# H3 convolution plus gated MLP, forward and gradients: the recorded order of all instructions and their PSUM banks replaced

## The chip, the cores and the metric

The kernel runs on one core of one Trainium2 chip. The metric is the time of one execution in device microseconds (us), given as the median over runs. One more execution is recorded by the hardware profiler, and views of its trace are quoted in what follows. A core has the engines PE (TensorE, matrix multiplies and transposes), DVE (VectorE), ACT (ScalarE), POOL (GpSimd) and SP (SyncE), which here issues all the DMAs; 16 DMA engines carry them.

## The reference

A token sequence x of length S = 2048 and width D = 512 (bf16) goes through a layer norm, and two blocks are added to it. Wanted are the result and its gradients for nine inputs. Shortened:

```
def _A_ref(q, k, v, shift_k, ssm_k, ssm_D):
    # k_shift: sum over t = 0..3 of k_pad[:, t:t+S] * shift_k[:, 3-t]
    kv = k_shift * v
    # FFTs of length 2S in float32 over the sequence
    y = irfft(rfft(kv_pad) * rfft(ssm_k_pad))[:, :S]
    return q * (y + kv * ssm_D)
def _B_ref(x, w_gate, w_up, w_down):
    return ((x @ w_gate) * (x @ w_up)) @ w_down

x = A_q
xn = _layernorm(x)
out = x + _A_ref(xn, A_k, A_v, A_shift_k, A_ssm_k, A_ssm_D) + _B_ref(xn, B_w_gate, B_w_up, B_w_down)
# returned: out, and the gradients of sum(out * grad_out) for A_q, A_k, A_v,
# shift_k, ssm_k, ssm_D, w_gate, w_up, w_down
```

The hidden width is F = 1376.

## The kernel before, in words

**Layout.** The sequence is held as 16 rows r of 128 tokens, one token on each partition. Nearly all of SBUF is one tile, `big`, in which every array has a fixed address; all of PSUM is one tile, `PP`, cut into eight banks. Therefore the profile calls nearly everything `big` or `PP`. Four arrays in DRAM carry results between stages: HD (products of the MLP), AX (first step of the transform), CX (spectral product) and KS (shifted k).

**How the order is made.** The kernel's text does not issue instructions itself. The engines are replaced by the wrapper `Eng` (lines 143 to 179), and each call is appended to a list `ops` of 2,285 recorded operations: 1,009 for PE (several matmuls can be one operation; 3,190 in all), 654 for DVE, 361 for ACT, 3 for POOL and 258 for SP. PSUM is asked for in 398 slots (`rF` for two banks, `rN` for one) without a place. At the end `emit(PLAN)` (lines 181 to 189, called on line 976) decodes the string PLAN of line 34: 2,285 numbers, the order in which the operations are really issued, and 398 numbers, the bank of each slot. Line 173 is the wrapper's inner line, so nearly every instruction of the profile carries L173. Each engine runs its own instructions strictly in the issued order; semaphores between engines follow from the data. The calls `at(t)` note a due time beside each operation; with a given PLAN they decide nothing. All DMAs are on SP's queue, so an SP instruction that waits holds up all later loads and stores.

**Stages, in the order of time.**

- Start (0 to 34 us): dummy matmuls (324 to 334), then loads, from 362 on: rows of x (`xload`), the transposed gradient goT (`gtload`), the first weights (lines 363 and 367; the other groups by `w_load`, 321), and the gradient `go` in four pieces of four rows (`gload`). `ln` (392) normalizes, `tr_rows` (406) transposes.
- `mlp_rows(j, r)` (416): for six column groups j of F and pairs of rows r, the product pd of go and W_down, the products with W_gate and W_up, and their pointwise products. These stay in a ring in SBUF and mostly go to HD (`hd_store`, 443). `dw_gen(j)` (582) makes the weight gradients of group j from them.
- `a_gen` (453): the shift convolution on DVE and the first step of the transform on PE, stored to AX. `s_gen` (`s_B` 514, `s_pw` 529, `s_Bi` 546): over the frequency blocks, loads of AX and of tables E into SBUF, the spectral products on DVE, the way back, stores to CX. Both are interleaved with the MLP, up to about 240 us.
- `turn_gen` (615): the last two column groups don't go through HD. They are transposed in SBUF, partly by eight DMAs (`ldT`, here called turn(r) by its row), partly by PE in groups numbered k = 0, 8, ... 88.
- `hd_load(n)` (642): a DMA transpose from HD, once for each n = 0 to 7.
- The late loop, n = 0 to 7, two rows each (from 240 us to the end; lines 935 to 975). For each n, `c_load(n)` (676) loads the block C from CX (1.5 MB), and `last_dft(n)` (719) is the last step of the transform on PE; `c_y` (729), `c_dkv` (737) and `c_o5` (755) work on its three results. `c_dsk` (764) forms products on DVE and adds them up on PE; `dk_pair` (710) is the transposed shift convolution, seven DVE operations and a store. `y_o(n, rr)` (784) is the MLP's last product for row 2n + rr, 11 matmuls with what `hd_load(n)` brought, added to the rows of x (`y_load`, 688), then a store of out. `y_x(n, rr)` (801) is 22 matmuls, the layer norm's gradient on DVE and ACT, and a store of the gradient of x. `k_load` (691) and `dkv_load` (682) bring rows of k, v and KS. `psd_end` (824) copies and stores the sums of `c_dsk`.

So there are three kinds of chains in the late loop: CX by DMA to `last_dft` and on to ACT and DVE; HD by DMA to `y_o` and `y_x` and on to DVE; and buffers of one or two turns, which a store must have left before DVE writes them again, and which a load must not overwrite before PE and DVE have read them.

The line that plays the recorded operations is this:

```
            for i in order:
                for fn in ops[i].fns:
                    fn()
```

Of the kernel before, what the change touches and what calls it, by code (L numbers as in the profile page):

```python
# [17 lines left out]
S = 2048  # L18
D = 512
F = 1376  # L20
R = 16
# [4 lines left out]
SB = [0, None, 1, 2, 3, 4]  # L26
# [4 lines left out]
RING = 28  # L31
RO = [0, 16, 24, 40, 56, 72]
EPS = 1e-5
PLAN = "c-l=@V-TK6vu*dpcCx|7wr$(C?G1Kgd$Swcwr$(Cv$pS>e1C2|T~jkXjdS{`nw|m307-zM7^Hwtpa>)YflN>w;zMFc2nflcC@2^>1c(ArAsUo`=nw-+LNbU6r6Cq1f>O{H+Cv$L4RIg`#D%g@4pPEOhzB`gCgg%u&<;94M@R*EAs;k@7Vs4$h1`%D@<S(R37Me)6ofo50=hs~C<Ha3Gc<w1&>WgVZRiHIpgYuoDliBpLtUr@RiPeKhEJgZ42CJt5Gp_`7z3lAA`FE3@EKHtk<bWwKzW!5LtrRWhuts<j=&<=1dZVf*aDx!XjlwmVHj+N*3bviz*gu93m`iThpCVWGvhYc4%1*E?15{L7<<7{NP;_|DkjBhI0L4`myis1z%Iyw)o}^*g{9CNYG79U4#vSUSPrwHAN(cX!W`%iE8uIG1#4k7T!M9w7LLL9Fc*G+bg%}}!wL8mqT@VR4?n_j7!N051MG(^Z~(5uDaeL<;U_o;w_qRKhU9n<Qs5!@1b>F?cp6gTWk`j;z<Ch-1|CCdOoJET23&+s@hYUn9GDK%<4wqbSKvNmgpBwQa^e$s1T`@iD&|JR2apy11xLVuwXilK=D{{l2kYYRkQbw1KFp8x@HeQB|3Lvf3s0dSM#To$5dVO?PzW30GHi^?aRsi#KcN|}!oQ(8w!oIy3ZFw0{0my+Mp%b2a2O89JMaS9U^HBfZLu9T#b?kSW8xazjeBqu#=;KR5j$aL9F1Kt4(>(98t@uk!an?4-auCzfv;d3#>Q+g690kq*d4p!J9rBda3YSu{Wu+a;3VvcYq1y3z}`3>Cu1KRi(lae{2Hg=0o;fOu`f==e%K#3;{d!%pV2^EfSd3$jEi65JRF1zaSjf~AvhNY(EvDtg>fbh#d|Ox2h)6LL7!thT!gc6F}9>xco^$bLM(y}s3<n11Q;J%QC%8BOR*8Pre@THwqQLvgdM3dHK(K4iHhMAI*!Hh1eU;(*q%z^G3-D?sSTCJQ<w<L;2AuRgctB4mc`R}7R%u!yo}{>8eYNA=?l7w74U1Sh}W<ZR>qUql&)hHyn#1yE5@W9cnfdi9lVRNs4abg_i!r3rZ^Or?&CCifDiE$#iK{~7^l-N+>TH1DL%valz^UNLP|t4=mmaBeJCa6q+B$RwqYttO)oJqy~0w|m(tKVEKM`%HNL?zl$-vPb~Kz$QywZyd8r)rpnUWe-{E^a14-ypN=xM_9aW&D^bLNCBPcy(pfmIx=BMv5BPF8(l!-D^Mfw4M#Gfz={fxihub7nzQa1VxlT#t8M8D%%`U4A7cKQ>0(l9zlJMl048~?!+^e_I0MW`rMreXwyM8s5ugeJfeR5Eg^N}o`mYV;LVrzljMa!^z%LD8r))u5VGlA==`I#08y3tgaE)Qx)49GXijX&&{at~8QX(J0zL>!=@%rh7Do)>D64N@M9hZKUP&fR@oXdPpm16Rn}~G?6CLCE87^X#(w}!?1_8(<7Qhn`sw)OIv6M?WG0u9qps7^dnuQh4d4hq{Xy|=F|7|10ACGaD*PyVR}k8=w~`gOXvXIrduTZ3q7Hmbdc^uNGgBIX_@&MrQ`Jck}_~cenHPE6ThO&{2Q&M%XE#7(eIRnv+{AeLfQB#W#_*r2mehu+4(iSrCdCS-_Uh>N4XjJJ;i0@cpQWCu<;)>nE#|9JdOXQp*)47@xSs9ea`<#dH#Z9a(o`f(K!ka=X^Yg$8rLW%9D9C$Ku#rfh+P<p3Y;q5+`KS{9J&?@kp-BLAQ}B=qOIai8=C%bUY{Ff?S2aq5q^17iQK8Jcq0DEGoiDxi-ZhQPo)-MU(MdPR`La1xM4bcs~{8VqBb~YE1o_XLAgVqn~g!j;9?tu9o1Gnvzp-Nsh0nwK~_}QXETTYbs66rMV0bpfsF76KYvbqcyo4C)Q6jktWr=T#Gw#60Oa3IISkvx|~kaYdub;ow*Bl<rLbD>vMO`rWv#WH{|TvgFn$YoL?JpPj1XjxGCpQf)SikoADyft@C*;H|LBxk8^2d{gT&l6>Y%<bOyKNUfhaX^J4DJRW-9_)jnKU7jhO|#+h^p=hfxBl>2f)t*Lpm9~aVE`jTI9F>S*ov@I9WqFP+nb8UUi8@QBK(;C{Hs%uFtqh+-}x8v)4gUe}Yy~($D0O!-&TwdGr9j>4abs*Q#N_v+&aAUp4_xS<8;YRw9D{3pPr*C-$KjH@Zm|N=;uCGt|8Mo0U`i`G-Gi|FK^gVyWb@f~Rj@xMxNh%Y$pElL@noK(B_uN90OA6_t1N0N=s4F?8^w-YXLkDYD9il^Z6Q`2YvW<Ic8ri|y`7{1hy6X=-P=Dl|oK|}4XWCr1@K2mh2I*G*TvzjM?xt(FmyXoYnnQMRHtD13rLT_CNt#_UNJ|}~Ipt^0DC2apZsaVIRWeB~`Gt$fuRK<#X;E3M$9SpcmJ@WGPw+`T#Y^-w57RSTLeBDV4KiJ)>aX;ruHq>=LTBiH4qQ^c(kL=ZqslTpzz2DzF4r$~g+`M(T1?LI0$r)&b%I8hLtI?u>3P1uG30Aqq-%7x9^sg>N-uJ0i6!%OweHqSyiot6b$Xc>@Lb)izwut)pjUVwU*+}sJ5SWuvPDbDF1^NE^$$MG+cb{kk!rF>YselxsClKj9M+n$QRB){-lPR&zi!ri5>F23K0TyYw6+}8{1RXO<bskwu4zIkEQw?@&*Z<jiX@h+dPFa3RoSk8^Cdm5JM|ylp=IQ<p3{H%g5J>cx>gIxX+5T8<*fe4C$xf`(sEK!&ge}ADK9PLme!J!`c!Xg6G3Sycl4Rw)$7_+?rCLtq0OY8G>}TtT<+@|eWI<TzBH7F`dDA-EqS1=<&nPA=Xy=P(Z~@ezv^xIUF*n8eZfD;Z+cyB$ZHk(PH)OvRry1ImcO*FbdkpLr@mK{HsaDw?#j2?NdDHJ^hdoT?IpAPqyOs9`ipjz|FoNQkQeg3{vtnUM*({&ZH276Jd@~#)<evmOEl{#Zk?o;^p==*PlB;M61Dph*E&ld=_@fz?199$I2P3&OB73E52c^PvtQ+vd}?X!H|Z|}WT3p3&m@)&l9V=BVp{@BXh$TqCABGXRE|j^J1(g#oh7#9c0x`{5=(DW<&-3|X);|h*eCWxGTLc5Be!jaq_DH{rR23tmf5mcew!&-?JGGaU(0!!CE0DZJhD7i(6U($`%W&%Qz>jYEuZDG&63;Z$U7M#cdV!tw{K*q+_H;uNebELGFRrw_i|Z&mn~A-idX@gFAJokeJjOmkzA2dcF(?$5?02_+Avux3+263w&Ai>s#tk@Y};hJRJ9SZM3zc9+aWt;nJkxTwnA1)4I3$=<c;i->bBoT%PMJOZ)J?EmI_wU#>zNpYvZMowX+E_QPxO%t8KewkL;D2*1<a3B&lVcY_j|)ovn_|ve|au*2+3rFZ<+y{bOBhzig1M_Jee@x^~yPTRl4<2c?J2vHG@A=2`>$LpI4FX=sgXj2)K7*3)`f6KiU{t(i5q7S_jF+B}<Yt!%8dwgtA(#@Q1aZ%^&2Ot3{Z(car6n{3bQds}TUtgrR6pKOh-wQsDyEw&}L&VIB3Hqe&Z6#L8$*&thQ%WSYMx2ZPGHrNoGZpUnfeP<7Cg$=ch_N8sI&GxN5x0klXKDU{+(vI6#w$<L+HrsAL+ZVROhS}Hl&W77z`@u%oP8(^z*(w`luWgr&w%={Hy|O))+SB+S_O~T<_fNf;UoiGREx33zkK)lCojko4cl8)v!ee@3KV?z<FFRtfJcD1f*#3)|pSGix*7JKD&*+)FfbX@;9@oJOdlJv$l{~(mv6B9)U9+s7!?XDbYwc&PnwRo;UfpYW3jf4QdjhZNZ!Ej#^Xt~eJ9tj-=mkBQ|7+<ymlyI{-pR{&XK(9`y|$mUgkIKjds9#3dAyG2^}1fv%XxWk;uXBI*Yi}K+>3Y@@9I;$qPO#@-p!|ZPw(#2y}eiU{@%a`_~)L|2l@=3;5V#__wX-#nEz+<yqOR7rM}8P^D#c$>w81*<-L8GkMITF&l~v=@8hd|tS|Sz-rR56IlE*deU!KI%l4(O@tHo(XL$?%%2)VWAMN9Pov-)jzQKq3L~rRE{k(nclYEyS@)y3_H~UN9<nw*9zw&*4(BJq<f9tdTtZ(tHe$Nm4LVxEceU88PZ~US!@<D#YkNPD)<vV?!&GiR<%uo9gU+mxdHs9gLeY-#O{l3R9`w9Qf&-elV-mmy$zv|aKR!AFu@aulVfAVww%wM~QTmHM>^e3J!gb+L2_Bi3Z#|;-eeR$+iLcH)_<Pje~{OA}mg**PUKlKbDYDf_N@VlNc{NkBIqVT6v$Qbr|lE5KLxbM-zKb|!t4!?S~AmKMp6+Q`Vf`*i#Mko+0{N>R@(vUr*4sFAy;a~sTlZ6<eU`QTnhFT$J$Pr40+M!*@8R~@Gp>C)Ua)tJxV#pKfg%Y7s$Q$a1j-hgB5K4tYAzvsR3Wr9aOz0G<gkqs{IAC2u*^nl54GlwzaK)}#xzHjM3Hd|S&@FTi<-_FAAxsI4!{|^gG!Ml?|1dR-3DZK4Fd%#$dWDvuXQ&>UgrQ-2=pDWYGs4)=DtsB5hCX3)7#9YHnPFJi5<UxGg{@&-=o_|$;bDB36^4WnVSX4Hz7Ffd>@X@!2;0MsaL}5Cg<)dY8J30(VM%Bm_JrGESLhcGhGk)QI2MkF<za7F5sHR8VP!ZGPKE_xRk$1Wg;QZtSRGD>x#3FK8198L;eJ>Y28FX>UKku6gv()nxEdaYIbm@)6b^*L;Zb-Ku7$_pe7GLoh9}`^I1<i<O<_%V8J>lA;YN5BE`-<NXt){HhKu2Scph$rOW{R8Gt|gU9yoGwW^oh{^GG`rj!cZzoy~>aNIr-O2@s(}#1nu$a({J>EI;Za5*f@R@z9vuBGEr;h~R@eL>^g&2u>VvMx%%#(p)26CXt)FC@Y%6hvptxMzVuK<ak1jq|=BQlVL=KE)cP{NJmGAKr&E^I7cQCEf|VNoIi-0VkG?kzKGDrj2}Q6eI)dO&PP%fffzCRIDRxBh){z6|9#N?Z#RPZBVYR%#v}Cu`j8ngQpO1K50oO%B3mD7<q-_>0W*K7P=rckC6UT~2okALBvQoLKU7rz4<RIx`T"
KB = 1024


# [1 line left out]
def kernel(  # L39
# [141 lines left out]
    def emit(plan):  # L181
        raw = zlib.decompress(base64.b85decode(plan))
        order = struct.unpack(f"<{len(ops)}H", raw[:2 * len(ops)])
        for s, b in zip(slots, raw[2 * len(ops):], strict=True):
            s.base = Q[b // 2] if s.n == 2 else halves[b]
        with tc.manual_schedule(engines={mybir.EngineType.PE, mybir.EngineType.DVE, mybir.EngineType.Activation, mybir.EngineType.Pool, mybir.EngineType.SP}):
# [3 lines that stand above are left out]
# [452 lines left out]
    def hd_load(n):  # L642
        a, b = hd_span(n)
        ldT(out=hdP[n % 2][:, :, 0:b - a], in_=HP[n, a:b])
# [290 lines left out]
    for n in range(NCH):  # L935
# [32 lines left out]
        else:  # L968
# [4 lines left out]
            if n + 2 < NCH:  # L973
                y_load(n + 2)
                hd_load(n + 2)
    emit(PLAN)

# [106 lines left out]
```

## Time and profile before

| what | value |
|---|---|
| median of 3 runs | 427.12 us (426.57 to 427.43) |
| the profiled execution | 426.92 us, its span 425.1 us |
| PE busy | 414.8 us, 98% of the span |
| DVE busy | 350.7 us, 82% |
| ACT busy | 257.8 us, 61% |
| DMA moved | 127.27 MB, mean 299 GB/s |
| granted PE clock | 1.00 of full speed |
| last matmul ends | 420.1 us |

The span is the time from the first to the last recorded event; the 1.8 us between it and the profiled execution's time lie outside the trace. "Busy" counts the time in which an engine executes something, without its waits for semaphores; SP has no busy time, since issuing a DMA isn't counted. A wait is put down to what released it: "PE PP L173 <- DMA big<-CX" is a wait of PE, writing to PP, for a load from CX into `big`. The chain is the list of work that ended last, followed backward from the last instruction, each piece with what released it.

### The profile page before, as it was taken

What the parts mean: (1) busy time and instruction counts of PE and PEld (TensorE: products, weight loads), DVE (VectorE), ACT (ScalarE), POOL (GpSimd) and SP (SyncE); (2) the same over time, 40 slices, a digit from 0 to 9 for tenths busy, and PEclk for the clock granted to TensorE, in tenths of its full rate; (3) what the DMA queues carried; (4) which work ended last, traced back from release to release, by engine and by line L of the source; (5) the groups of instructions that cost most, each with busy time, mean ns of one, the idle gap of its engine ahead of it and who ended that gap; (6) DMA issues with size and microseconds to landing.
All of it is one profiled execution on the core that took longest, in us unless ns stands there. A gap on an engine that the chain in (4) does not pass through costs nothing.

```text
span 425.1 us, 8146 instructions
## 1 busy us (share of the span) xinstructions
PE 414.8 (98%) x3190; PEld 198.9 (47%) x3190; DVE 350.7 (82%) x684; ACT 257.8 (61%) x364; POOL 3.5 (1%) x9
## 2 busy tenths in 40 slices
PE   7999999999999999999999999999999999999995
PEld 4745555854554333544444334444444444444343
DVE  5999977998649989899999980325858898999996
ACT  4855988598644999888999953363414230422323
POOL 1000000000000000000000000000000000000000
PEclk9999999999999999999999999999999999999999
DMA  8999899999788879969889899999999999999953
GB/s 277 399 180 395 295 305 395 344 363 360 298 297 304 320 250 338 310 202 341 305 286 349 291 313 314 250 392 309 188 296 305 308 258 333 309 303 290 278 174 147
DMA packets 104222, 127.27 MB, mean 299 GB/s; under 512 B 63860, under 2 KB 73977, under 8 KB 103160
## 3 DMA queue, kind: packets, MB, share of 16 engines
q1 hardware_dynamic: 104184, 126.75, 94.4%
q8 instruction: 25, 0.41, 0.4%
q14 instruction: 13, 0.11, 0.1%
HBM read 57.10 MB, written 54.04 MB: 261 GB/s over the span
## 4 chain that ended last, share of the span: by engine, by line
PE 70%; DVE 14%; DMA 11%; issue 2%; ACT 2%; SPq 1%; ACTq 0%
PE PP L173 70%; DVE big L173 14%; DMA out_dram<-big 4%; DMA big<-CX 2%; DMA big<-in_k_dram 2%; ACT big L173 2%; SPq L173 1%; DMA big<-in_w_dram 1%; DMA big<-in_go_dram 1%; DMA big<-in_x_dram 1%; ACTq L1080 0%
## 5 line engine op out<-in xcount | busy, mean ns | idle before, releaser
L173 PE MATMUL PP<-big 128*128 128x512 bf16 (+7 forms) x3190 | 414.8, 351 | 5.3 <-DVE big L173 1.8
L173 DVE TENSOR_TENSOR big<-big 128x1024 bf16<-128x1024 bf16 (+2 forms) x465 | 268.1, 630 | 45.8 <-ACT big L173 36.7
L173 PEld LDWEIGHTS <-big 128*128 128x128 bf16 (+3 forms) x3190 | 198.9, 97 | 221.0 <-issue 64.4
L173 ACT CAST big<-PP 128x512 bf16<-128x512 f32 (+2 forms) x314 | 224.3, 781 | 87.1 <-PE PP L173 75.5
L173 ACT ACTIVATE big<-big 128x512 bf16<-128x512 f32 (+3 forms) x30 | 19.1, 642 | 50.1 <-DVE big L173 50.0
L173 DVE CAST big<-PP 128x512 bf16<-128x512 f32 (+1 forms) x37 | 32.4, 875 | 9.7 <-PE PP L173 5.1
L173 ACT COPY big<-PP 128x1024 bf16<-128x1024 bf16 x15 | 15.0, 1012 | 20.9 <-PE PP L173 20.8
L173 DVE SCALAR_TENSOR_TENSOR big<-big 128x1 f32<-128x1 f32 (+2 forms) x52 | 25.3, 499 | 0.3
L173 DVE SCALAR_TENSOR_TENSOR big<-big,PP 128x512 f32<-128x512 bf16 x14 | 9.6, 682 | 8.6 <-PE PP L173 8.6
L173 DVE BATCH_NORM_STATS2 big<-big 128x6 f32<-128x512 bf16 x16 | 10.5, 683 | 3.7 <-DMA big<-in_x_dram 3.7
L173 DVE TENSOR_TENSOR big<-big,PP 128x512 bf16<-128x512 bf16 x14 | 9.2, 681 | 1.1 <-PE PP L173 1.1
L173 DVE TENSOR_SCALAR big<-big 128x1 f32<-128x1 f32 (+1 forms) x28 | 6.8, 256 | 0.0
L173 POOL MEMSET big<- 128x1536 bf16 (+2 forms) x3 | 2.9, 950 | 252.3 <-PE PP L173 252.3
L173 ACT ACTIVATE big<-PP 128x512 f32<-128x512 f32 x2 | 1.2, 597 | 4.5 <-PE PP L173 4.5
L173 DVE BATCH_NORM_AGGREGATE big<-big 128x2 f32<-128x6 f32 x16 | 2.3, 169 | 0.1
L173 ACT ACT_TABLE_LOAD x1 | 1.3, 1283 | 0.7 <-PEq L1072 0.7
L173 DVE RECIPROCAL big<-big 128x2 f32<-128x2 f32 (+1 forms) x9 | 1.2, 151 | 0.6 <-ACT big L173 0.6
L173 DVE DVE_READ_ACCUMULATOR big<-big 128x1 f32 x16 | 1.3, 82 | 0.0
L173 DVE DVE_READ_ACCUMULATOR big<-big,PP 128x1 f32 x14 | 1.1, 81 | 0.0
L173 DVE MEMSET big<- 128x128 bf16 (+1 forms) x2 | 0.2, 112 | 0.8 <-PEq L1072 0.8
L173 DVE COPY big<-PP 128x1024 bf16<-128x1024 bf16 x1 | 0.7, 692 | 0.2 <-PE PP L173 0.2
L173 ACT ACTIVATION_READ_ACCUMULATOR big<-PP 128x1 f32 x2 | 0.4, 194 | 0.0
(6 smaller groups left out, 0.9 us busy)
## 6 DMA issues: line engine op xcount, KB each, us to landing
HD<-big SPq DMA_DIRECT2D x32, 384.0 KB, 5.8
AX<-big SPq DMA_DIRECT2D x16, 768.0 KB, 5.6
big<-AX SPq DMA_DIRECT2D x16, 768.0 KB, 5.5
CX<-big SPq DMA_DIRECT2D x16, 768.0 KB, 5.1
out_dram<-big SPq DMA_DIRECT2D x44, 256.0 KB, 3.5
big<-CX SPq DMA_DIRECT2D x7, 1536.0 KB, 8.3
big<-in_vK_dram SPq DMA_DIRECT2D x8, 512.0 KB, 5.3
big<-in_w_dram SPq DMA_DIRECT2D x4, 768.0 KB, 7.4
```

Of the source, the lines that this page charges most:

```text
L173: o.fns.append(lambda: f(*[fix(x) for x in a], **{kk: fix(x) for kk, x in k.items()}))
```

## The change

One line differs, the string PLAN (here cut after 60 characters of some 5,000):

```
-PLAN = "c-l=@V-TK6vu*dpcCx|7wr$(C?G1Kgd$Swcwr$(Cv$pS>e1C2|T~jkXjdS{`...
+PLAN = "c-lQ!W7wWYupZCGPGehbY&EuxHnyF#aT?pUZ6}Rw+fHqt_scog`LX-VHG9v@...
```

Decoded, the two strings hold the same 2,285 operations in two orders. The orders on PE, ACT, DVE and SP differ; that of POOL's three operations doesn't. 299 of the 398 PSUM slots have another bank. Operations, operands, SBUF addresses, tile shapes and the queue of each DMA are the same, and the large stages follow each other as before; what differs is the place of single operations within some microseconds on each engine. On average an operation stands 2.7 us of work from its old place on PE, 1.9 us on DVE and 1.6 us on ACT. The largest shifts:

- At the start SP issues x(2), goT(3), x(1), the first part of the weights, goT(1), x(0), goT(4, 5) and so on (numbers are rows, or pairs of rows for goT); before, x(2), x(6), goT(4, 5), x(0), D, the weights. One of the four pieces of `go` comes 17th instead of 27th. The first products on PE are pd of `mlp_rows` for r = 6 and r = 2; before, the transposes of row 2.
- PE's transposes of `turn_gen` come later: groups k = 32 to 64 by 16 to 35 us, 80 by 64.5, 88 by 78 us.
- `y_o(5, 0)` and `y_o(6, 1)` come later on PE (by 7 and 12 us of work). The last piece of PE's work is `c_dsk(7)`. The sums of `y_o(3, 0)` and `y_o(5, 0)` on DVE come later by 6.9 and 10.6 us.
- On SP, `hd_load(2)` stands four places earlier and `c_load(3)` seventh behind it instead of fifth; the store of `y_x(1)` and the DMA transpose turn(8) stand just ahead of `hd_load(4)`, the latter instead of just behind it; turn(14) goes from the 244th place to the 224th.

2 lines of the change are left out of this document (1 added, 1 removed).

## The prediction

> **What bounds the kernel now.** I read, in this order, the totals, the waits of each engine, the table by stage, the chain, and SP's instructions in order of time. The first two say that TensorE is nearly full and that its visible waits are short (after the name: us in total, times, longest):
>
> ```profile
> span 425.1 us, 8146 instructions
> PE 414.8 (98%) x3190; PEld 198.9 (47%) x3190; DVE 350.7 (82%) x684; ACT 257.8 (61%) x364; POOL 3.5 (1%) x9
> ```
> ```profile
> PE PP L173 <- DVE big L173: 1.8, 2, 1.1
> PE PP L173 <- DMA big<-CX: 1.7, 2, 0.9
> PE PP L173 <- DMA big<-in_w_dram: 0.9, 1, 0.9
> PE PP L173 <- DMA big<-in_go_dram: 0.6, 1, 0.6
> ```
>
> In the trace PE stands still for about 1 us at 6.8 (w), 32.2 (go), 335.8 (C), 363.1 (DVE), 380.2 and 395.2 (C); its matmuls without those and smaller gaps take 413.4 us. I count PE by this nominal time, and by its lag, the real time less the nominal one: 3.8 us from 34 to 300, then 4.6, 5.2, and 6.6 at the end. A new order can win nearly only from this lag, and can lose anything.
>
> ```profile
> 180.00:240.00 60.00, 60.00 (x615) 25.62 (x614) 59.42 (x111) 55.98 (x72) 0.00 (x0) 1.00 0.85 302
> 270.00:285.00 15.00, 15.00 (x99) 7.05 (x99) 4.98 (x8) 7.77 (x11) 0.00 (x0) 1.00 1.09 338
> 360.00:380.00 20.00, 19.27 (x112) 8.37 (x110) 20.00 (x44) 5.76 (x7) 0.00 (x0) 1.00 1.10 328
> 380.00:400.00 20.00, 18.93 (x138) 8.09 (x138) 19.93 (x43) 7.29 (x8) 0.00 (x0) 1.00 1.13 279
> ```
>
> In this table by stage (window; us, then busy of PE, weight load, DVE, ACT, POOL; clock, DMA share, GB/s) DVE has two thirds of a stage free at 270–285 and nothing from 360 on, and the DMA engines are full throughout the late loop. Per pass of that loop PE needs some 16 us, DVE 17.9, and SP's queue this:
>
> ```profile
> 372.84 10.67 SPq L173 DMA_TRANSPOSE big<-HD  x1
> 383.56 1.48 SPq L173 DMA_TRANSPOSE big<-big  x1
> 385.13 2.37 SPq L173 DMA_DIRECT2D out_dram<-big  x4
> 387.60 0.72 SPq L173 DMA_DIRECT2D big<-CX  x1
> 388.37 0.64 SPq L173 DMA_DIRECT2D big<-in_vK_dram  x1
> 390.65 0.33 SPq L173 DMA_DIRECT2D big<-in_x_dram  x1
> 391.08 9.50 SPq L173 DMA_TRANSPOSE big<-HD  x1
> ```
>
> The eight hd_loads (transposes from HD) hold SP for 7.3 to 10.8 us each, a plain issue for about 0.45. The trace also shows eight DMAs in flight at most: the issue at 336.8 comes with the landing, at 336.7, of the one eight before it. So three engines are within 2 us of each other, and the late end is set by SP's order: the chain ends with c_load(7), 387.60 to 396.42, then 23.7 us of PE without a gap, and 5.0 us of tail.
>
> **The change, part by part.** It is a permutation: no instruction is added or removed, all durations stay, so every term is a wait. The sum is against the profiled execution (426.92 us; span 425.1, 1.8 outside it), which is 0.20 below the median. I decoded both orders and laid the durations of before on the new one.
>
> *Start (0–34).* the first part of w_load(0) goes to SP's fourth place instead of its sixth, 896 KB of loads up to and with it instead of 1,409; the rows of go that stalled PE at 32.2 go 17th instead of 27th; the first real matmuls are pd of mlp_rows for r = 6 and 2. This takes the two stalls of 1.08 and 0.96 away; the later x(6) and x(8) give some 0.7 of new waits by the loads' landing rows. So PE is −1.3 at 34 us (bounds −2.0 and 0). What is late next is C in the late loop, which hangs only partly on PE, so I let −0.5 of it reach the end.
>
> *Middle (34–270), with the banks.* PE is busy 66.00 of 66, 80.00 of 80 and 60.00 of 60. Placed in the new order with the old times, s_B(0) comes 1.0 to 1.6 us before its E and X are ready near 126, and a bank that has changed asks in some ten places for an ACT copy 0.1 to 0.6 us too early. Most is made good by ACT's own shift. Nothing here could be gained, as there are no stalls left. I take +0.5 (0 to +2). On banks the Trainium skill ("Perfetto Trace Analysis", Matmuls) has independent groups rotate through different banks so that evacuation overlaps. Of the 398 slots 299 change bank and both orders rotate over all eight; by the rule this term would be 0, and the sum 0.5 lower.
>
> *Turn transposes, later.* The PE transposes of turn_gen that are in groups k = 32 to 64 go 16 to 35 us back, k = 80 and 88 64 and 78 us, each 0.45 us. PE then reaches the late items 2 to 4 us of work sooner: last_dft(3) at a nominal 314.3 instead of 316.6, (5) 356.7 for 358.8, (6) 370.8 for 374.5, (7) 388.5 for 389.9, y_x(7,0) 395.2 for 399.3. That would be a gain if PE could start them. But before, last_dft(3) started 0.29 us behind the landing of its C, and last_dft(4) 0.04 behind. So the gain turns into waits for C and HD.
>
> *SP, late.* I walked SP's new order with 0.45 per issue, the old holds, and landings by nearest rows (2.3 to 2.8 us behind an hd_load, 8.3 for a C load, 11.6 for hd_load). hd_load(2) stands four places earlier and goes at 298.9 instead of 300.8, c_load(3) comes seventh behind it instead of fifth. Issue times: c_load(3) 310.2 (before 311.7), hd_load(4) 341.4 (338.8, since a store that waits for DVE and the DMA transpose turn(8) now stand ahead of it), hd_load(5) 358.6 (358.0), c_load(6) 369.6 (368.2), hd_load(6) 373.4 (372.6), c_load(7) 387.0 (387.4), hd_load(7) 391.1 (390.8). The lag that each landing asks of PE: hd_load(4) 6.4, hd_load(5) 6.6, c_load(6) 7.2, hd_load(6) 6.9, c_load(7) 396.0 − 388.5 = 7.5, hd_load(7) 7.5. The end lag is then 7.5 instead of 6.7: +0.8, PE's end at 420.9 instead of 420.1. In other words, c_load(7) lands 0.4 sooner, but 24.9 us of PE work follow it instead of 23.5.
>
> *Heads of the queue.* Each hold could slip: the y_o(3) store (its DVE work goes back 6.9 us) stands ahead of hd_load(5), the y_o(5) store (back 10.6) ahead of hd_load(7). At 360–400 DVE has nothing free to catch up with. Behind those hd_loads on SP wait C and k for the next pass. My walk has 5 us of room for the second and about none for the first. Bounds 0 and +5; I take +0.9, a quarter of the 3.5 us by which the holds themselves differ, as the rows are nearest to no slip. On these holds a rule speaks against counting them: the Trainium skill ("DMA: Bandwidth & Descriptors", Issuing engines are not separate DMA queues) says the sequencer's time to initiate a DMA "is usually small relative to the DMA itself". The rows disagree (9.50 of some 11.6 us). By the rule this term would be 0, and the sum 0.9 lower.
>
> *DVE and tail.* One product of c_dsk(0) (1.28 us) goes into the hole at 270–285, and c_y's last product waits less for the y_x store (2.0 us at 320.6), so DVE is 1.5 to 2 us ahead at 322 and 0.9 when the x rows of y_load(3) gate it. PE's last item is c_dsk(7), behind it an ACT copy of the sums and a small store; DVE's chain for the last y_x ends about 0.6 sooner. Tail 4.6 instead of 5.0: −0.4 (−1.0 to +0.5).
>
> Sum: −0.5 + 0.5 + 0.8 + 0.9 − 0.4 = +1.3, so 428.2 against the profiled run and 428.4 against the median.
>
> **The rivals.** *Faster:* DVE, not SP, sets the late end. DVE is 90 to 100% busy there, and its lead of 1.5 to 2 us at 322 would then pass to the end, with the stores and hd_loads that wait for it. It decides at whether y_load(3) lands before 335 (my walk: 336.9). Against it stands the chain, which ends over C. −2 us: 425.1; chance 0.30. *No change (within 0.2%):* the C loads hold both orders to the same end; +0, 427.1; 0.18. *Much slower:* the store ahead of hd_load(4) or (5) waits for DVE, the hd_load slips by 2 to 3 us twice, and as SP has 8.3 + 7.2 + waits of each 17.9 us, it doesn't come back: +4 to +6, 432; it decides from a slip of 2 us, the room that DVE's lead gives; 0.20. *That the change does nothing:* all four working queues differ and 299 banks; only POOL's three operations keep their order. Left out.
>
> **How the numbers follow.** The forecast, 428.4, has 0.32; its own range is 427.9 to 429.5. A measurement can tell about 0.2% (0.85 us) from no change: faster 0.30, same 0.18, slower 0.52. The range takes in most of the faster case, down to 424.9, and of the much slower one up to 432.5; about a fifth is left outside.
>
> **What would show it.** Start: PE's waits for w and go gone from its list, PE ahead by about 1 us at 34. Middle: PE busy under 80.00 of 80. Late: PE's waits for C and HD longer (4 us or more instead of 1.7), hd_load(4) issued at 341 or later, the chain ending over C or HD. Tail: 4.6 us. I am wrong if DVE's waits shrink and PE's lag at last_dft(7) is under 6.6 (the faster case), or if SP's wait for DVE just ahead of an hd_load is over 2 us (the much slower one).

## The result, and the profile after

| what | before | after |
|---|---|---|
| median | 426.85 us (4 runs beside it) | 440.27 us (4 runs) |
| ratio | | 1.0307, interval 1.0273 to 1.034 |
| the profiled execution | 426.92 us, span 425.1 | 439.03 us, span 437.2 |
| last matmul ends | 420.1 us | 433.4 us |
| from there to the end | 5.0 us | 3.8 us |

The kernel became 13 us slower, outside the range of the prediction, and the profiled executions differ by 12.1 us. PE ends 13.3 us later; the tail gave 1.2 back. Executions that were disturbed (one of after's four) are left out of the ratios, and changes in microseconds are worked out from the ratios, though the medians hold them.

The page's totals of after:

```profile
span 437.2 us, 8074 instructions
PE 414.5 (95%) x3132; PEld 200.7 (46%) x3190; DVE 359.1 (82%) x684; ACT 257.4 (59%) x364; POOL 3.5 (1%) x9
```

The instructions are the same (58 matmul records are missing from this trace, hence x3132). ACT's busy time is as it was, but DVE's is 359.1 instead of 350.7 us with the same 684 instructions. That line turned out to be the key to a part of the loss. PE's waits over the whole span (us in total, times, longest):

```profile
PE PP L173 <- ACT big L173: 6.4, 7, 1.9
PE PP L173 <- DMA big<-CX: 4.1, 3, 2.7
PE PP L173 <- issue: 2.1, 12, 0.3
PE PP L173 <- DVE big L173: 1.7, 3, 1.1
PE PP L173 <- DMA big<-in_go_dram: 1.3, 1, 1.3
```

The first line is new: before, the list has no wait for ACT. The stage from 180 to 240 us, whose row of before the prediction shows, is now this (window; us, then busy of PE, weight load, DVE, ACT, POOL; clock, DMA share, GB/s):

```profile
180.00:240.00 60.00, 59.01 (x596) 26.85 (x607) 57.78 (x102) 53.40 (x70) 0.00 (x0) 1.00 0.79 277
```

In 180–240 PE, DVE and ACT all do less than before in the same time, so none of them is simply fuller: they hold each other up. The same table has the stage that lost most ahead of 240, first before, then after:

```profile
100.00:180.00 80.00, 80.00 (x703) 35.32 (x701) 65.95 (x109) 61.34 (x81) 0.00 (x0) 1.00 0.87 311
```
```profile
100.00:180.00 80.00, 76.84 (x642) 33.67 (x652) 65.67 (x106) 58.20 (x78) 0.00 (x0) 1.00 0.84 299
```

By PE's lag (the prediction's measure: real time less nominal time of the matmuls issued so far) the loss is spread. After less before is +0.5 us at a nominal 30 us, +2.2 at 100, +4.5 at 220, +8.2 at 250, +8.1 at 270, +10.4 at 320, +14.1 at 330 and +13.3 at the end. So about a third arises up to 220, more than a quarter in one short stretch (a nominal 220 to 250; in real time 244 to 261 us), and the rest between a nominal 285 and 330, which is about 298 to 349 us in real time. From SP's queue around its last two hd_loads, answering the list shown of before (start, us, what):

```profile
387.68 8.59 SPq L173 DMA_TRANSPOSE big<-HD  x1
400.44 0.41 SPq L173 DMA_DIRECT2D big<-CX  x1
404.02 9.04 SPq L173 DMA_TRANSPOSE big<-HD  x1
```

hd_load(7) goes 13 us later than before, and c_load(7) 12.8: the late loop as a whole is shifted. The chain no longer ends with 23.7 us of PE behind c_load(7). Behind a last piece of PE it ends with 26 us of DVE alone (408 to 434 us), of which the first piece stands here, so DVE, not a load, closes the kernel:

```profile
403.10 4.92 PE PP L173 x22
408.05 2.40 DVE big L173 x6
```

### The profile page after: what moved, and what is told of

It reads as the page before. It is cut to its first block, busy times and chain, and to the rows that moved or that the text cites. A ratio compares the mean times of both kernels' runs of the same rounds, so it can differ in the third digit from the quotient of the medians.

```text
span 437.2 us, 8074 instructions
## 1 busy us (share of the span) xinstructions
PE 414.5 (95%) x3132; PEld 200.7 (46%) x3190; DVE 359.1 (82%) x684; ACT 257.4 (59%) x364; POOL 3.5 (1%) x9
## 5 line engine op out<-in xcount | busy, mean ns | idle before, releaser
L173 PE MATMUL PP<-big 128*128 128x512 bf16 (+8 forms) x3132 | 414.5, 352 | 18.9 <-ACT big L173 6.4
L173 DVE TENSOR_TENSOR big<-big 128x1024 bf16<-128x1024 bf16 (+3 forms) x465 | 275.0, 632 | 48.6 <-ACT big L173 35.9
L173 PEld LDWEIGHTS <-big 128*128 128x128 bf16 (+4 forms) x3190 | 200.7, 98 | 232.2 <-issue 70.1
```

Of the source, the lines that this page charges most:

```text
L173: o.fns.append(lambda: f(*[fix(x) for x in a], **{kk: fix(x) for kk, x in k.items()}))
```

## The experiments

In these tables a change in microseconds is (ratio − 1) × 427 us. All kernels have the same instructions, except where it is said. "Pairs" is a count from the decoded orders, explained under the fifth group.

### 1. Which half of the order costs

The first question was where the loss arises: in both halves (theory A), or nearly all in the late loop, as the prediction had its losses (theory B). early_new takes the new order and banks for the first 1,448 operations (to 231 us) and the old ones behind; late_new is the reverse; loop_new begins the new order only at 281 us.

```
early_new:  order = after[:1448] + [o for o in before if o not in after[:1448]]
late_new:   order = before[:1448] + [o for o in after if o not in before[:1448]]
loop_new:   the same as late_new, cut at 1755
```

> The new order and banks for the first 1,448 operations (to about 231 us of before), the old ones from there on; the cut is at a place where both orders have issued the same operations on every engine. Theory A (waits on PE add up, since PE has no free time anywhere): the lag of PE at the cut is 5 us over before and stays, so about +5, 432. Theory B (the late loop is held by its loads, so an early slip is taken up there): +0 to +2, 427 to 429.

> The other half: old order and banks up to the same cut, the new ones after it. Theory A: the rest of the loss, +8, about 435. Theory B: nearly all of it, +11 to +13, 438 to 440.

> Old order and banks for the first 1,755 operations (to about 281 us of before), new ones after, so only the late loop is new. Theory A: the +3 that PE's list shows at 231 to 281 of the new kernel is not in it; left are the wait for the transposed blocks (2.0), the wait for C of n = 4 with the halved clock behind it (3.0 + 1.8), less 1: about +5 to +6, 432 to 433. Theory B: +8 or more, 435.

Measured: early_new 433.57 us (1.0142, 1.0104 to 1.018): +6.1. late_new 431.47 (1.0119, 1.0065 to 1.0173): +5.1. loop_new 429.04 (1.0053, 1.0037 to 1.007): +2.3. early_new is as theory A had it. late_new is under both prices and loop_new under half of its, so both theories made the late half too dear. The two halves add up to 11.2 of 13.1, so most of the loss is local to each half; the 1.9 us left over are less than the intervals are wide, and may be nothing. Half of the loss comes from the early stages, which the prediction had put at nearly nothing. loop_new is close to what the prediction said of the late part alone, and its SP queue follows the prediction's walk (these times are counted, as the walk's are, from a zero 0.2 us behind that of the profile's rows): c_load(3) goes at 310.3 us (walk 310.2), hd_load(4) 342.0 (341.4), hd_load(5) 359.5 (358.6), c_load(6) 370.6 (369.6); only hd_load(6), c_load(7) and hd_load(7), at 376.4, 390.0 and 394.7, miss it, by 3.0 to 3.6.

### 2. The banks, and SP's order alone

banks_only keeps the order of before and gives 320 of the 398 slots other banks. new_spold is the kernel after with SP's own sequence of before; old_spnew is the kernel before with SP's sequence of after.

```
banks_only: order = before;  banks = others, still free when each slot needs them
new_spold:  PE, ACT, DVE, POOL, banks = after;   SP = before
old_spnew:  PE, ACT, DVE, POOL, banks = before;  SP = after
```

> The old order on all engines, 320 of the 398 slots in other banks, chosen so that no slot waits longer for its bank by the old times. If the number of a bank matters by itself: some us slower. If only the distance between two users of a bank matters (theories A and B both): 427, within 0.2%.

> The new order on PE, ACT, DVE and POOL and the new banks, but SP's queue in the old order, over the whole kernel. Theory A1 (the loss of the first half sits between PE and ACT, that of the late loop in SP's order): the first half keeps its +6, the late loop loses little: about +6 to +7, 433 to 434. Rival (the new order of PE itself asks for C and HD too early, whatever SP does): +10 or more, 437 to 440.

> The complement: the old order and banks on PE, ACT, DVE and POOL, only SP's queue in the new order. Theory A1: nothing in the first half, the late loop pays the late stores and the late C loads: +4 to +7, 431 to 434. Rival: within 2 us of before, 427 to 429.

Measured: banks_only 428.11 us (1.0023, 0.9994 to 1.0051), no clear effect. new_spold 480.01 (1.1226, 1.1172 to 1.128) and old_spnew 462.71 (1.0827, 1.076 to 1.0893): all theories were wrong by nearly 30 us and more. SP's order can't be exchanged alone. In old_spnew the engines wait for what now stands behind something else on SP: DVE 14.6 us for stores of out, 11.3 for rows of x and 7.9 for KS (in before 2.2, 4.6 and nothing), and ACT 18.2 us for stores, of which before has none. SP's own waits are long in every kernel and hardly tell the two apart (81 to 85 us for each of DVE, PE and ACT, in before 71 to 78). A queue with stores and loads in one line must have the order in which the engines produce. So these two runs say nothing about the change, and the question "is it SP or the engines" has no answer of this kind.

banks_only shows less than its name says. Its banks were chosen to be free when the old order needs them, so it shows that the number of a bank costs nothing. Whether the banks of after are as good for the new order was not tried. The trace of early_new gives a hint that they are not quite: between 34 and 241 us PE waits six times for ACT, 2.9 us in all, where before has no visible wait of PE, and five of these waits (2.6 us) end with the copy that empties the bank which PE writes next. That is the very thing for which the prediction had looked, in "some ten places".

### 3. One exposed head, and PE's clock

In late_new and after, ACT's copy of `c_o5(1)` waits 8.8 and 7.9 us for the store of `c_o5(0)`, and the copy of the turned group k = 8, for which PE waits, stands behind it. late_turn8 exchanges the two in late_new. new_fill adds 26 matmuls to after, whose results nobody reads, into PSUM slots that PE is about to wait with, so that the pauses are not idle.

```diff
 ACT, late_turn8:
-c_o5(1) copy;  turn_gen k=8 copy
+turn_gen k=8 copy;  c_o5(1) copy
 PE, new_fill:
+ahead of y_x(1): 8 matmuls 128x512; last_dft(4): 12; last_dft(6): 6
```

> The kernel late_new with one exchange on ACT: the copy of the turned group k = 8 goes ahead of c_o5(1)'s copy, which in late_new waited 8.8 us for the store of c_o5(0) while PE's y_x for row 1 waited 2.9 us for the copy behind it, with a halved clock after that. Theory (one late store on SP, through the head of ACT's queue, to PE): that wait and the low clock after it go, 2 to 4.5 us less than late_new, 427.5 to 429.5. Rival (PE meets the next late load instead): within 1 us of late_new, 430.5 to 432.5.

> The new kernel with 26 more matmuls of 128x512 on constants, into PSUM slots that the next operation overwrites: 8 ahead of y_x for row 1, 12 ahead of last_dft(4), 6 ahead of last_dft(6), where PE stood still for 2.05, 3.0 and 1.4 us; they take 1.7, 2.6 and 1.3 us. Theory (a pause of PE of some 2.6 us halves its clock for 3.4 us, which costs 1.7 us beyond the pause): clock 1.00 in these stretches and 1 to 2 us less than the new kernel, 438 to 439. Rival (the pause alone costs): no gain or a small loss, 440 to 441.

Measured: late_turn8 432.52 us (1.012, 1.0085 to 1.0156), no gain on late_new's 1.0119. The wait that was aimed at (2.8 us of PE, for ACT) is gone; PE's waits between 280 and 350 us, in late_new and then in late_turn8:

```profile
PE PP L173 <- DMA big<-CX: 3.7, 2, 2.5
PE PP L173 <- ACT big L173: 2.8, 1, 2.8
```
```profile
PE PP L173 <- DMA big<-CX: 4.4, 2, 2.5
PE PP L173 <- DMA big<-HD: 0.9, 1, 0.9
```

By its lag PE is 3.6 us earlier at a nominal 300 us, but only 1.2 us at 330: the loads of C and HD give it little to do sooner. So the outcome is the rival's: by itself this head costs nothing that can be told.

new_fill: 440.18 us (1.0268, 1.0202 to 1.0335), single runs from 435.7 to 442.4, inconclusive. What it was after is a thing that the profile after shows (345 to 351 us; the clock is the last figure but two, 1.00 is full speed):

```profile
345.00:347.60 2.60, 0.12 (x4) 0.00 (x0) 1.91 (x6) 0.00 (x0) 0.00 (x0) 1.00 0.90 340
349.00:351.30 2.30, 1.97 (x18) 0.65 (x12) 2.22 (x5) 1.65 (x2) 0.00 (x0) 0.50 1.03 395
```

PE waits 2.7 us for c_load(4), and then the granted clock is 0.50 for 3.4 us, which costs another 1.7 us. With new_fill that dip is gone, but another came at 108 to 111 us, behind a pause of 2.4 us at 104 us that the page of after doesn't have.

### 4. Counting the dips of PE's clock

The dips can be counted without a trace, since every execution lists its mean clock: one dip of 3.4 us at 0.50 takes 0.4% off the mean. loop_new's ten executions have 1.000 (two: 427.8 and 428.3 us), 0.998 (428.8) or 0.995 and 0.996 (seven: 428.3 to 430.1, mean 429.3). The two without a dip are 1.0 us above before, the seven 2.4. So of loop_new's 2.3 us more than half goes with the dip, which fits the 1.7 us that one costs; the longest wait for C in its trace is 2.6 us. In late_dve_apart_2 (below), the three of twelve executions at 0.998 or more take 427.4 to 429.2 us, and the three at 0.992 or less 431.1 to 434.1.

### 5. DVE's own order: operations that depend on the one just ahead

The start times of DVE's instructions in the traces fall in two classes. An instruction that depends on nothing of the one just ahead starts 0.083 us before that one's end. One that reads or overwrites its result, or overwrites what it reads, starts 0.034 us behind its end (medians of 526 and 69 neighbours in before, of 459 and 130 in early_new). I call such a dependent neighbour a pair; it costs 0.083 + 0.034 us, unrounded 0.118. In after each of them waits for DVE's own semaphore, which the instruction just ahead raises; 90 others wait for the same semaphore, but for an earlier instruction, and start 0.082 us before the end of the one ahead all the same. So it is not the semaphore as such that costs, but having to wait for the instruction just ahead. Here are five products of one size in a row, `a_gen` at about 81 us: in before with a second chain laid between them, so that each is independent of its neighbour (first line), and in after, where `TT(tmpA, ...)` and `TT(ks, ks, tmpA)` (lines 461 and 462) follow each other directly (start, us for all five):

```profile
80.77 3.10 DVE L173 TENSOR_TENSOR big<-big 128x1024 bf16<-128x1024 bf16 x5
```
```profile
80.49 3.60 DVE L173 TENSOR_TENSOR big<-big 128x1024 bf16<-128x1024 bf16 x5
```

Four neighbours cost 0.50 us, 0.125 each, while one instruction alone takes 0.685 and 0.692 us. before has 75 pairs, after 169, early_new 136, late_new 108, loop_new 99: the new order runs each chain of `a_gen` and `s_pw` in one piece where the old one laced two together. This was theory D: the pairs lengthen a DVE that is full. Four kernels change only DVE's order, by moves of a few places.

```diff
 after_dve_apart, s_pw of block 3 and 4 (the lines' numbers; the other moves are like it):
-543 i=3;  536 i=3;  541 i=3;  544 i=3;  532 i=4;  mlp_rows 436;  mlp_rows 435;  533 i=4
+536 i=3;  543 i=3;  541 i=3;  532 i=4;  544 i=3;  mlp_rows 436;  533 i=4;  mlp_rows 435
 before_dve_pairs:
-461 a_gen t=2;  436 mlp_rows(2, 0);  464 a_gen;  435 mlp_rows(2, 0);  462 a_gen t=2
+461 a_gen t=2;  462 a_gen t=2;  436 mlp_rows(2, 0);  464 a_gen;  435 mlp_rows(2, 0)
```

> The kernel after, in which only VectorE's own order is changed: 290 of its places, no operation by more than 9, so that an operation seldom stands directly behind the one whose result it reads or overwrites (15 such neighbour pairs instead of 169). TensorE, ScalarE, GpSimd, SyncE and all PSUM banks stay as in the kernel after. Theory D (a VectorE operation starts 0.034 us after the end of the one ahead when it depends on it, and 0.083 us before that end when it does not, so each pair costs 0.118 us): 154 pairs fewer are 18 us of VectorE's time over the kernel and about 9 to 10 us of it in the stretches where VectorE is full or releases ScalarE, so the time falls by 6 to 10 us, to 430-434, and VectorE's busy time falls from 359 to 345-352. Rival (the time went to banks, ScalarE's queue behind stores and late loads, VectorE's length does not matter): the order of the other engines is what it was, so 438.5-441, within 2 us of the kernel after.

> The same done to early_new (new order up to 231 us, old behind it; 433.6 us): 239 places of VectorE's order changed, none by more than 6, 12 dependent neighbour pairs instead of 136. Theory D: most of early_new's 6 us against the kernel before come from its 61 extra pairs, and the 12 us that 124 fewer pairs take off VectorE bring it back to 426-429. Rival: stays at 432-435.

> The kernel before, in which only VectorE's order is changed the other way: 221 places, none by more than 8, so that 170 dependent neighbour pairs stand in it instead of 75 (31, 36, 35, 43, 8 and 17 of them up to 34, 100, 180, 240, 285 us and the end; the kernel after has 13, 35, 39, 27, 14 and 41). All other engines and the banks stay as before. Theory D: 95 pairs of 0.118 us are 11 us of VectorE's time; ahead of 240 us, where nearly all of them lie, 5 to 10 us of it reach the end, so 432-437. Rival: no instruction, size, bank, load or store differs and every operation keeps its place to within 8, so 426-428.

> The kernel before with VectorE's 75 dependent neighbour pairs brought to 9 by moves of at most 7 places in its order alone. Theory D: 66 pairs of 0.118 us are 7.8 us of VectorE's time, of which only what lies on a full VectorE counts (26 pairs between 100 and 240 us and 17 behind 285 us): 424-426.5, a version faster than both kernels. Rival: VectorE's length does not matter, 426.5-427.5.

In these four, one to three products of `mlp_rows` read an array after it was filled again, so a part of the gradients has other numbers; the instructions and their sizes are the same.

Measured: before_dve_pairs 436.26 us (1.0204, 1.017 to 1.0237): +8.7, as theory D said. after_dve_apart is at 1.0259 (1.0213 to 1.0304), about 438.1 us: −2 against after, nearest its rival. early_dve_apart 432.07 (1.0117, 1.0067 to 1.0168): −1.1 against early_new, within the rival's numbers. before_dve_apart 426.51 (0.9989, 0.9959 to 1.002): no change that can be told.

So pairs alone can make before that much slower. An operation that had been moved ahead of its input would be another cause, but there is none: up to 245 us DVE waits 21.3 us in before_dve_pairs, and 24.3 in before. Its page has the very DVE time of after, and its PE and DVE lost in 180–240 what they lost in after:

```profile
PE 419.2 (96%) x3190; PEld 199.9 (46%) x3190; DVE 359.1 (83%) x684; ACT 258.4 (59%) x364; POOL 3.5 (1%) x9
```
```profile
180.00:240.00 60.00, 57.40 (x580) 25.23 (x570) 57.86 (x101) 52.37 (x68) 0.00 (x0) 1.00 0.77 284
```

But taking them out of after gave back little. One possible reason is seen in early_dve_apart's DVE between 79 and 86 us (start, us, what, and in brackets the idle time ahead and its releaser):

```profile
78.80 1.90 DVE L173 TENSOR_TENSOR big<-big 128x1024 bf16<-128x1024 bf16 x3
83.89 2.23 DVE L173 TENSOR_TENSOR big<-big 128x1024 bf16<-128x1024 bf16 x4 [3.19 <-DMA big<-in_vK_dram]
```

My move put a product of `a_gen` (464) five places ahead, to where its row of v had not landed, and DVE stood still for 3.19 us with ready work behind it. A part of the pairs' gain may have been spent there; the next group, which was to have no such moves, is the test of that.

### 6. The same, meant to put no operation ahead of its inputs

The second set moves an operation only where the traced run leaves room on both sides: not ahead of the landing or the end of what it reads, and not behind what its reader can bear. The computation is unchanged.

```
pairs:  after 169 -> after_dve_apart_2 46;   early_new 136 -> early_dve_apart_2 35
        late_new 108 -> late_dve_apart_2 36; before 75 -> before_dve_apart_2 29
```

> The kernel after with VectorE's dependent neighbour pairs brought from 169 to 46, and now only by moves (220 places, none by more than 9) that put no operation ahead of the time at which its inputs came in the traced run, nor later than its reader can bear. Theory D: 123 pairs of 0.118 us are 14.5 us of VectorE's time, 5 to 8 us of which reach the end: 432-436. Rival (the pairs are not what costs the new order its time; it is loads, stores and banks): 438-441.

> The same with early_new (433.6 us): 136 pairs brought to 35, 188 places changed. Theory D: 428.5-431, since VectorE's 12 us less take away most of the 5.5 us by which TensorE fell behind between 60 and 230 us. Rival: 432-435.

> The same with late_new (old order up to 231 us, new behind it; 431.5 us): 108 pairs brought to 36, 136 places changed, most of them behind 240 us. Theory D: VectorE is full from 360 us on, so 2 to 3 us of the 5 come back: 428.5-430. Rival (the late half is set by the loads of C and HD and a ScalarE copy behind a store): 430.5-432.5.

> The kernel before with 75 pairs brought to 29 by 97 places, none by more than 4, on the same terms. Theory D: 46 pairs are 5.4 us of VectorE's time, of which 1 to 2 us show: 425-426.5. Rival: as before, 426.5-427.5.

| kernel | us | ratio, interval | against its parent |
|---|---|---|---|
| after_dve_apart_2 | 438.29 | 1.0268 (1.0234 to 1.0303) | −1.7 us |
| early_dve_apart_2 | 430.88 | 1.0096 (1.0062 to 1.013) | −2.0 us |
| late_dve_apart_2 | 430.36 | 1.0067 (1.0035 to 1.01) | −2.2 us |
| before_dve_apart_2 | 426.74 | 0.9994 (0.9969 to 1.0019) | (before) −0.3 us |

Theory D was too large: for after it expected 5 to 8 us and got 1.7, within the rival's numbers; the early half came out as theory D had it, the late half between the two, before as the rival had it. The intervals of parent and child overlap in all three, so each of these gains is likely rather than shown. The traces bear out the early one: against before, PE falls 2.6 us further behind between a nominal 100 and 220 us in early_new, and 0.1 us in early_dve_apart_2. For after the second set gave back no more than the first (1.7 and 2 us).

At one place the moves were not what they were meant to be. In after_dve_apart_2 and early_dve_apart_2 another product of `a_gen` (464, g = 3) comes to the head of DVE's queue before its row of v has landed, and DVE stands still from 63.7 to 66.7 us with ready work behind it: 2.9 us, where this product waits 0.3 us for v in after and 1.4 in early_new. So what parting alone is worth isn't shown cleanly in these two.

The law of the pairs itself holds well. DVE's busy time goes with their number in every kernel with this instruction list:

| kernel | pairs | DVE busy, us |
|---|---|---|
| before_dve_apart | 9 | 345.8 |
| before_dve_apart_2 | 29 | 346.9 |
| after_dve_apart_2 | 46 | 349.6 |
| before | 75 | 350.7 |
| loop_new | 99 | 352.9 |
| late_new | 108 | 353.8 |
| early_new | 136 | 356.3 |
| after | 169 | 359.1 |
| before_dve_pairs | 170 | 359.1 |

From 9 to 170 pairs it grows by 13.3 us, 0.083 us for each: just the overlap that a pair loses (the other 0.034 us is idle time). What theory D missed, as far as the traces show, is that DVE's length was one of several holds. ACT's waits for DVE, from 34 to 241 us, rose from 3.0 us in before to 11.1 in after, and in before_dve_pairs they are 12.1. In order, these three kernels:

```profile
ACT big L173 <- DVE big L173: 3.0, 4, 1.8
```
```profile
ACT big L173 <- DVE big L173: 11.1, 11, 2.3
```
```profile
ACT big L173 <- DVE big L173: 12.1, 10, 3.1
```

early_new has 11.1 us in 11 such waits, and with the pairs parted, early_dve_apart_2 still has 12.1 us in 12: in the new order these waits don't come from the pairs alone. What stands at the head of ACT's queue is the next thing to look at.

### 7. Three heads of queues

What was left in after_dve_apart_2 showed three single places. ACT's copy of `mlp_rows(2, 4)` waits 2.2 us at 69 us for DVE's product of row 0; in after and in early_new this wait is 0.7 us, so most of it came with the moves that parted the pairs: DVE's product that waits for v stands ahead of it. ACT's copy of pd of `mlp_rows(2, 14)`, whose bank PE needs, stands behind a copy of `a_gen` that waits 1.4 us (in early_dve_apart_2) for the store of AX row 9; after has this wait too (1.5 us), early_new doesn't. And near 256 us, in the whole new order alone, two copies of `s_Bi` wait for stores of CX. That one in after, ACT from 250 to 262 us:

```profile
250.05 3.89 ACT L173 CAST big<-PP 128x1024 bf16<-128x1024 f32 x6 [0.89 <-PE PP L173]
258.11 1.01 ACT L173 CAST big<-PP 128x1024 bf16<-128x1024 f32 x1 [4.17 <-DMA CX<-big]
259.93 1.01 ACT L173 CAST big<-PP 128x1024 bf16<-128x1024 f32 x1 [0.81 <-DMA CX<-big]
```

The two copies for block i = 7 write the array that the stores of i = 6 must have left. These are issued at 251.1 and 252.0 us, and the second lands at 259.9, 7.9 us behind its issue. In after a part of c_load(0) and rows of WY stand just ahead of them on SP, loads whose data are not needed for 20 us and which land up to 256.1 us; SP then waits some 7 us more, for ACT, before it can issue the stores (the last line):

```profile
238.56 1.64 SPq L173 DMA_DIRECT2D big<-in_wy_dram  x2
242.40 0.33 SPq L173 DMA_DIRECT2D big<-CX  x1
242.78 0.42 SPq L173 DMA_DIRECT2D big<-in_wy_dram  x1
243.25 0.44 SPq L173 DMA_DIRECT2D big<-in_k_dram  x1
243.73 0.44 SPq L173 DMA_DIRECT2D big<-CX  x1
251.09 1.29 SPq L173 DMA_DIRECT2D CX<-big  x2
```

In before the stores of i = 6 are issued at 243.0 and 243.9 us and land by 249.4 us at the latest, 5.5 us behind the issue, and ACT doesn't wait for them.

```diff
 DVE, both kernels:
-464 a_gen g=3;  461 a_gen g=4;  436 mlp_rows(2, 0);  462 a_gen g=4;  435 mlp_rows(2, 0)
+436 mlp_rows(2, 0);  435 mlp_rows(2, 0);  461 a_gen g=4;  464 a_gen g=3;  462 a_gen g=4
 ACT, both kernels:
-481 a_gen copy, row 13;  429 mlp_rows(2, 14) copy
+429 mlp_rows(2, 14) copy;  481 a_gen copy, row 13
 SP, after_heads alone:
-wy_load(1, 11);  k_load(0);  c_load(0), part;  store CX;  store CX
+k_load(0);  store CX;  store CX;  wy_load(1, 11);  c_load(0), part
```

> early_dve_apart_2 (430.9 us) with two small moves: VectorE's products mlp_rows(2, row 0) stand two places further ahead, for which ScalarE's copy at 69 us waits 2.2 us and TensorE 1.3 us, and ScalarE's copy of mlp_rows(2, row 14), whose bank TensorE waits for 1.1 us at 105 us, stands ahead of the copy that waits for the AX store of row 9. Theory E (what is left of the early loss is a few heads of engine queues): 428-429.5. Rival (the wait moves to the next head, as when the turned group was moved): 430-431.5.

> after_dve_apart_2 (438.3 us) with the same two moves, and on SyncE's queue the loads of WY (1, 11) and a part of C(0) behind the stores of CX that two ScalarE copies at 256 us wait 5.6 us for; TensorE waits 3.4 us there and its clock is then halved for about 3.4 us. Theory E: the pause at 256-260 us goes with its clock (5 us) and 1 to 2 us of the early heads: 431-435, nearer 434 if a load of C that is now later takes some of it. Rival: the late part waits for its loads anyway (c_load(4) at 349 us, 3.4 us), so an earlier arrival there only waits longer: 436.5-439.

Measured: early_heads 428.47 us (1.0047, 1.0017 to 1.0077), −2.1 against early_dve_apart_2, in the range of theory E. The two intervals overlap, so this gain too is likely rather than shown, and part of it takes back what the parting had brought (the 2.2 us at 69 us, and with it DVE's wait for v). In the traces PE is 1.5 us ahead of early_dve_apart_2 at a nominal 220, but the two spans, 428.6 and 428.8 us, are nearly the same. Both sets of moves together are clear of noise: −4.1 against early_new, whose interval (from 1.0104) lies wholly above this one (to 1.0077). after_heads 435.54 (1.0208, 1.0174 to 1.0242), −2.6 against after_dve_apart_2, less than theory E's lower price and more than the rival's. ACT in after_heads loses nearly all of the wait (ACT, 246 to 258 us), and the second store now lands 5.5 us behind its issue (248.9 to 254.4):

```profile
246.98 3.89 ACT L173 CAST big<-PP 128x1024 bf16<-128x1024 f32 x6 [0.88 <-PE PP L173]
253.08 1.01 ACT L173 CAST big<-PP 128x1024 bf16<-128x1024 f32 x1 [2.21 <-PE PP L173]
254.42 1.01 ACT L173 CAST big<-PP 128x1024 bf16<-128x1024 f32 x1 [0.33 <-DMA CX<-big]
```

PE's lag, less that of before, grows by 2.6 us from a nominal 220 to 270, where in after_dve_apart_2 it grew by 6.2. Of these 2.6, 2.2 us are a new wait (272.9 to 275.0 us): PE stands at last_dft(0) for the last part of c_load(0). The page puts it down to no releaser ("issue"), but the load's landing at 274.95 us ends it. This is not the part that was moved back: its place on SP is the old one, and it reads what the stores of i = 7 write, which land at 270.0 us, just before it is issued. So PE, which comes sooner, waits for the next late load, as the rival said of c_load(4).

## Why the prediction was wrong

It forecast +1.3 us and got +13.1. The step that failed is **"Middle (34–270), with the banks"**, with +0.5 us (0 to +2): there PE fell 7.6 us behind (its lag less that of before went from +0.5 at a nominal 30 us to +8.1 at 270), and the early half alone costs +6.1 us. Under it lies a premise that failed too, **"It is a permutation: no instruction is added or removed, all durations stay, so every term is a wait"**: DVE is busy 8.4 us longer with the same instructions.

- *Start, −0.5.* Wrong in sign, by little. At a nominal 30 us PE is 0.5 us later than in before, instead of 1.3 us earlier. The stall for w went, as said; the one for go did not (1.3 us instead of 0.6), and a wait of 1.1 us for DVE stayed.
- *Middle, +0.5.* Wrong by an order of size. The error was to lay old durations in the new order one by one. On a single operation DVE's durations did stay, 0.69 us. The time between two of them didn't: 94 pairs more are 94 × 0.118 = 11 us of DVE's time in a kernel where DVE is full in 180–240, at 59.42 of 60 us, a row that the prediction itself shows. I had read that row as "nothing could be gained", and not as "nothing may be added". But the 11 us are a price on DVE, not what reached the end. before_dve_pairs shows that 95 pairs alone can cost 8.7 us; taking 123 out of after gave back only 1.7, though with a new wait of 2.9 us for v; with that undone and two more heads exchanged, after_heads is still +8.9. So pairs explain a part of after's loss, and the larger part is waits at single places and, in part, open. The Trainium skill ("VectorE: DVE Perf Modes", The DRAIN you can't avoid) says that the next operation doesn't start until the pipe is empty and that leaving out the semaphore between operations gains nothing, by which the order would change nothing on DVE and this term would be nil; it adds that an operation that isn't held starts earlier, without a price. The two rows of five products, 3.10 and 3.60 us, agree only with the addition.
- *Middle, the banks.* banks_only bears the prediction out for the numbers of the banks alone. For the new order it isn't shown: PE's 2.6 us of waits for emptied banks in early_new are of the kind that the prediction named and held to be made good, and they don't fit the nil that it drew from the Trainium skill's rule on rotating banks.
- *Middle, the heads.* The second half of the same step's error: "Most is made good by ACT's own shift." early_heads shows two heads, on ACT behind a store and behind DVE, whose exchange gave 2.1 us: likely rather than shown, and partly on a wait that the parting had made longer. The copies at 256 us are of the kind that the prediction did look for on SP ("Heads of the queue"), but only behind hd_loads, not for a store of CX behind loads. There after's PE falls 3.7 us behind between a nominal 220 and 250.
- *Late gates, +0.8, and heads, +0.9.* About right by themselves, too small for after. With the old early half loop_new is at +2.3; its queue goes by the walk to within 1.0 us up to c_load(6), and then slips by 3.0 to 3.6 us, inside the bound of 5. But what the walk could not hold is that a wait of PE of about 2 us and more can also halve the clock behind it (1.7 us each); it can, and need not. In after PE loses another 5.2 us of lag behind a nominal 270 (from 8.1 to 13.3), three times the 1.7 us of the two terms, with the wait for c_load(4) and its dip in it. Waits for C of 4 us or more were foretold as the sign and came (4.1). The Trainium skill's rule ("DMA: Bandwidth & Descriptors", Issuing engines are not separate DMA queues) would make the holds of hd_load small beside the transfer; 8.59 and 9.04 us of SP in after speak against it, as in before.
- *Tail, −0.4.* Right in sign; 3.8 us instead of the 4.6 foretold. The end is now set by DVE, the condition that my "faster" rival named, and it came true without being faster.
- *The rivals.* The much slower one came nearest in sign and size, but by another mechanism: no store that waits for DVE let an hd_load slip by itself; the late loop was already 8 us late when it began.

How the 13 us divide, as far as shown: the early half 6.1, of which parting the pairs and exchanging the two heads take back 4.1 in early_heads against early_new, whose intervals don't touch, about half by each step, of which the second also undoes the wait for v; the late half 5.1, of which parting the pairs seems to take back 2.2; what is left, 1.9 us, can't be told from nothing. after_heads, with all of it, is still +8.9. **Open** is most of that. The rest of the early half, 2.0 us, is spread over the start and a few short waits. In the late half PE's wait for c_load(4) stayed in every run that has the new order there from 231 us on: 2.0 to 3.1 us, with the half clock behind it in after, late_turn8 and late_dve_apart_2. In loop_new, whose new order begins at 281 us, it is only 0.8 us, and what the difference comes from wasn't looked for. In after last_dft(3) is done with the block ahead at 330.3 us, but c_load(4) is issued only at 339.6, right behind hd_load(3), which holds SP for 9.2 us from 329.7, and a store of out; no run moved it ahead of them. Why 72 pairs fewer in late_dve_apart_2, 8.5 us by the price and 5.2 in DVE's busy time, give back only 2.2 us wasn't tried either, nor other banks for the new order.

No version was faster than the kernel before; before_dve_apart_2 ties with it at 0.9994.

## What to carry to other kernels

"The same instructions in another order" isn't "the same busy time": count, on each full engine, how often an operation depends on the one just ahead of it, and lace two chains together where they do; but only if nothing is pulled ahead of its input, since one head wait of 3.19 us, as in early_dve_apart, is as long as 27 such pairs. When a reordered kernel gets slower, read the busy times for a change first, then cut the order in halves; then look for single heads, in particular loads without hurry issued just ahead of a store whose buffer is waited for. Removing one exposed wait tells only whether it bound at that moment: late_turn8 removed 2.8 us and gained nothing that can be told.

## What the runs showed of the hardware

- VectorE: an instruction independent of the one ahead starts 0.083 us before that one's end, a dependent one 0.034 us behind it. That is 0.118 us, or 0.125 by the two rows of five, of 0.69 us for one instruction of 128x1024. It was measured where the dependent one waits for VectorE's own semaphore, raised by the one ahead; a wait for it on account of an earlier instruction cost nothing (90 in after).
- TensorE's clock: visible pauses of 1.89 us (late_turn8, 319.5), 2.28 (late_new, 383.5), 2.47 (late_turn8, 339.0), 2.61 (loop_new) and 2.68 us (after) were followed by 3.4 us at 0.50; pauses of 2.30 us (new_spold, 99.8), 2.48 (late_new, 340.3) and 3.08 us (after_dve_apart_2, 345.9) were not. So the length alone doesn't decide here. The Trainium skill ("TensorE: Matmul & The Clock Gate", Why this matters for your kernels) advises no idle gaps over about 3 us; here 1.9 us were enough once, and 3.1 us were not. Its figure for the window, 3.4 us (What's actually happening), agrees with the length of the slow stretch.
- SP's queue: given the other order's sequence, the same instructions on all engines take 35 us more (old_spnew against before) and 39 more (new_spold against after).
